# Attention's end, the MLP's first and its last period: bit steps, sums, splits and second-layer products in another order

## The chip, the core and the metric

One core of a Trainium2 chip runs the whole program in one launch. The metric is the time of one execution in microseconds of device time, the median of several runs. The engines have queues of their own and run in the order in which their instructions were written down: TensorE (PE in the profile) multiplies matrices, VectorE (DVE) and ScalarE (ACT) read what it leaves in PSUM, GpSimd (POOL) works on SBUF alone here, and SyncE (SP) issues the transfers. They wait for each other by semaphores that are set when the program is built.

## What is computed

Clustered attention, then a gated layer (MLP), then a mixture of four experts. The part that the change touches is the border between the first two and the whole of the gated layer:

```
x    = attention output, 1536 tokens x 512
gate = 1 / (1 + exp(-(x @ w_gate)))          w_gate, w_val: 512 x 1536, given in float64
val  = x @ w_val
y    = (gate * val) @ w_out                  w_out: 1536 x 512, float64
then   out = sum over 4 experts of p_e * (relu(y @ w1[e]) @ w2[e])
```

## The kernel before, in words

Every number that TensorE multiplies is split into a high part (rounded to fp32r) and a low part, the rest; a product is high x high + high x low + low x high. ACT mostly makes the high part by a copy and POOL or DVE the low part by a subtraction (`split`). The float64 weights come as pairs of 32-bit words. ACT takes a scaled magnitude of the upper word and converts the lower one (`mag`, L687 and L689), DVE does three bit steps (`bits`: clamp L694, shift L695, merge of the sign L696), and POOL adds the rounding (`round`, L701).

The gated layer runs in six periods p (NP = 6) of 256 hidden columns, for the batches b = 0 and 1. One gate or one value product of a 512 x 256 weight block with a batch's 512 x 768 operand is done by seven products of half-size blocks in place of eight (`seven`, L810 to 868), which need four sums of weight blocks (`sums`, L736) and four sums of operand blocks (t1 to t4). They are issued in the order 1, 6, 7, 5, 2, 4, 3, six matmuls of 384 columns each. There are four PSUM banks for them: product 1 and later 2 lie in the first, 6 and later 4 in the second, 7 in the third, 5 and later 3 in the fourth. L843 (u2) reads the second bank and sets it free for product 4; L851 reads the fourth and lets product 3 add to it; L860 and L865 finish products 4 and 3. The results leave in `evict`: for the gate a sigmoid on ACT (L902), for the value a multiplication by the gate on DVE (L914), then the high part G on ACT (L915) and its low part on POOL (L916). The second layer, `outp` (L920 to 962), multiplies G with two outer blocks of w_out (`part`, L925 to 929), f = 0 and 1, into four banks per half n of a batch, and adds each to acc (L937 to 941). With `soon` its first half interleaves the four banks.

Between two steps of a `seven`, and behind every evict of an `outp`, stands a place for other work: the lists given to `gate`, `value` and `outp` in `moe1` (L966 to 1046) are taken one entry per place, and so set by hand the order on ACT, DVE and POOL. In attention the same is done by tables, of which TAIL (L73) holds the steps behind the last of the 96 score blocks' places: the number is the place, counted back from the end. In it `t1` is the first operand sum of batch 1 (POOL, L554, tile tB), `bits10` and `bits11` are the bit steps of the two halves of the first value weights (tile cv), `round10` and `round11` their roundings, `xadd6` and `xscale6` add and scale the last but one pair's output (POOL, L534 and L538, tile R), and `sums1` and `t2` follow. In the last period `ys` and `ysplit` (`operands`, L1053 to 1068) make the four sums and the seven splits of the mixture's first operand, out of acc: sums on DVE (L1066), high parts on ACT (L1063), low parts on DVE (L1064).

Of the kernel before, what the change touches and what calls it, by code (L numbers as in the profile page):

```python
# [28 lines left out]
def r2(ap):  # L29
# [48 lines left out]
    "table": (-3, 2),  # L78
# [3 lines left out]
class Net:  # L82
# [801 lines left out]
    def moe1(self, xadd, xscale):  # L884
        nc = self.nc
        NP = F1 // 256
# [33 lines left out]
        def outp(p, b, work=(), soon=False):  # L920
# [3 lines left out]
            def part(ps, d, c, f, some=range(3)):  # L924
                dc = slice(d * 128, d * 128 + 128)  # L925
                t = self.outers[2 * p + f]
                for k in some:
                    x, y = (("hi", Gh), ("lo", Gh), ("hi", Gl))[k]
                    nc.tensor.matmul(ps, t[x][:, dc], y[:, f, c], start=f == 0 and k == 0, stop=f == 1 and k == 2)  # L929
# [16 lines left out]
            for n in range(2):  # L946
                c = slice(n * HB, n * HB + HB)
                if soon and n == 0:
                    banks = [bank() for _ in range(4)]
                    for some in ((0, 1), (2,)) if p in (0, NP - 1) else (range(3),):  # L950
                        for d in range(4):
                            part(banks[d], d, c, 0, some)
                    for d in range(4):
                        part(banks[d], d, c, 1)
                        evict(banks[d], d, n)
                else:
                    for d in range(4):
                        ps = bank()
                        part(ps, d, c, 0)
                        part(ps, d, c, 1)  # L960
                        evict(ps, d, n)
# [14 lines left out]
        def total(u):  # L976
            return [lambda: u["sums"](Q)]
# [8 lines left out]
        split0(2, V)  # L986
        gate(0, 0, [[vs[0], o0["split"]], [vs[1]] + d[0], [vs[2]] + d[1], [vs[3]] + d[2], d[3] + d[4], [], [xadd, xscale]])
        go = load(U[1][0])
# [5 lines left out]
        c, d = conv(U[1][0], 0), conv(U[1][0], 1)  # L994
        gate(0, 1, [c[0], c[1], c[2], c[3] + c[4] + d[0], d[1] + d[2], d[3] + d[4], total(U[1][0])])
        outers[2]["load"]()
        value(0, 1, [load(U[1][1])] + [[go] for go in U[1][0]["split"]])
        for p in range(1, NP):
# [18 lines left out]
            outp(p, 0, [d[0], d[1], d[2], d[3] + d[4], total(g), [split[0]], [], [split[1]]], soon=True)  # L1017
            value(p, 1, [load(U[p + 1][1]), [split[2]], [split[3]]])
        f = 2 * NP - 1
# [3 lines left out]
        self.load_in2(0)  # L1023
        c, e = conv(o0), conv(o1)
        outp(NP - 2, 1, [[vs[1], vs[0]], [vs[2]] + c[0], c[1], c[2], c[3] + c[4], [vs[3]] + e[0], e[1] + e[2], e[3] + e[4]])
        self.load_out2(0)
        self.load_in2(1)
        value(NP - 1, 0, [[o0["split"]], [o1["split"]]])
        out, cin = self.conv_out2(0), self.conv_in2(0)
# [7 lines left out]
        ys, ysplit = self.operands(0, [room(self.opx, t, F32) for t in ("h1", "l1", "h2", "l2")])  # L1037
        gate(NP - 1, 1, [[ys[0]], [ys[1]], [ys[2]], [lambda: ysplit(0)], [], [], [lambda: ysplit(4)]])
        Y[6] = room(self.xp, "tA"), room(self.xp, "tB")
        value(NP - 1, 1, [[cin[1]], [cin[2], lambda: ysplit(5)], [], [], [], [], [ys[3], lambda: ysplit(3)]])  # L1040
        self.late2 = late = self.conv_in2(1)
# [234 lines left out]
```

## Time and profile before

| what | value |
|---|---|
| median of 3 runs | 1051.17 us (1050.76 to 1051.79) |
| the profiled execution | 1050.76 us, its span 1048.8 us |
| TensorE | 1030.3 us busy, 98% |
| VectorE | 815.6 us, 78% |
| GpSimd | 626.0 us, 60% |
| ScalarE | 542.7 us, 52% |
| granted TensorE clock, mean | 0.996 of full speed |

The span runs from the first to the last instruction; the execution's time holds some 2 us more around it. Busy shares are means over stages of different kinds: attention ends at about 258 us, the gated layer lies between there and 545 us, and the mixture behind it. Where TensorE is busy nearly all the time, another engine's work matters where TensorE waits for it.

### The profile page before, as it was taken

How to read it: one execution, taken by the hardware profiler on the slowest of the kernel's cores; microseconds unless marked ns; L12 is line 12 of the kernel's file. 1: busy time of each engine (PE TensorE's matmuls, PEld its weight loads, DVE VectorE, ACT ScalarE, POOL GpSimd, SP SyncE). 2: the span in 40 equal slices, each digit the busy share in tenths (PEclk: the TensorE clock that was granted, in tenths of full speed). 3: DMA queues.
4: the chain of work that ended last, by engine and by line, in shares of the span. 5: the costliest groups of instructions: out<-in, count | busy, mean ns of one | idle time of the engine just before them, and what ended most of it. 6: DMA issues, size and time to landing. Idle time of an engine off the chain costs nothing.

```text
span 1048.8 us, 16255 instructions
## 1 busy us (share of the span) xinstructions
PE 1030.3 (98%) x5817; PEld 963.0 (92%) x5817; DVE 815.6 (78%) x1418; ACT 542.7 (52%) x1147; POOL 626.0 (60%) x577
## 2 busy tenths in 40 slices
PE   7999999998999999999999999999999999999998
PEld 7899999998999999999999899899899889989987
DVE  7899999899887777787787776776777876676675
ACT  5889989889654444444344333333343433333320
POOL 6676777988576868676758444444444644444430
PEclk8999999999999999999999999999999999999999
DMA  9668978563122222222212221221213221221201
GB/s 197 148 157 190 209 163 180 140 166 94 51 62 66 74 82 60 62 61 65 77 41 81 81 68 55 81 81 41 81 61 122 81 81 44 77 81 61 61 21 61
DMA packets 86544, 95.96 MB, mean 91 GB/s; under 512 B 42752, under 2 KB 59488, under 8 KB 86464
## 3 DMA queue, kind: packets, MB, share of 16 engines
q1 hardware_dynamic: 86320, 94.89, 34.0%
q8 instruction: 46, 0.75, 0.3%
q14 instruction: 34, 0.28, 0.1%
q10 hardware_dynamic: 144, 0.03, 0.0%
HBM read 65.07 MB, written 3.19 MB: 65 GB/s over the span
## 4 chain that ended last, share of the span: by engine, by line
PE 84%; DVE 6%; POOL 4%; issue 2%; ACT 2%; SPq 1%; DMA 0%; DVEq 0%; POOLq 0%; ACTq 0%
PE ph L830 34%; PE po L1143 8%; PE po L1144 8%; PE po L1142 8%; PE po L929 7%; PE S L456 5%; PE T L476 5%; PE PV L489 3%; PE PV L490 3%; PE sn L311 1%; PE sT L293 1%; PE T L269 1%; POOL G L916 1%; DVE ph L865 1%; DVE sg L914 1%
## 5 line engine op out<-in xcount | busy, mean ns | idle before, releaser
L1098 POOL TENSOR_TENSOR wol<-r,woh 128x512 fp32r<-128x512 f32 x62 | 80.1, 1294 | 151.9 <-ACT woh L1097 151.7
L1149 DVE SCALAR_TENSOR_TENSOR acc<-po,pn,acc 128x512 f32<-128x512 f32 (+1 forms) x181 | 129.8, 742 | 36.2 <-PE po L1144 36.2
L1144 PE MATMUL po<-woh,h2l 128*128 128x512 f32 (+1 forms) x374 | 145.6, 389 | 0.0
L1143 PE MATMUL po<-wol,h2h 128*128 128x512 f32 (+1 forms) x374 | 145.6, 389 | 0.0
L1142 PE MATMUL po<-woh,h2h 128*128 128x512 f32 (+1 forms) x374 | 145.0, 388 | 0.0
L748 POOL TENSOR_TENSOR w1l<-sf,w1h 128x512 fp32r<-128x512 f32 x88 | 114.9, 1326 | 43.5 <-ACT w1h L745 43.3
L1117 ACT ACTIVATE h2h<-ph 128x384 fp32r<-128x384 f32 x128 | 62.5, 490 | 119.5 <-PE ph L830 93.4
L830 PE MATMUL ph<-h,w1h 128*128 128x384 f32 x336 | 113.8, 339 | 1.2 <-ACT sg L902 0.6
L830 PE MATMUL ph<-h,w1l 128*128 128x384 f32 x336 | 112.7, 336 | 0.0
L830 PE MATMUL ph<-l,w1h 128*128 128x384 f32 x336 | 112.6, 335 | 0.0
L480 DVE TENSOR_TENSOR pl<-T,ph 128x384 fp32r<-128x384 f32 x192 | 97.6, 549 | 16.7 <-ACT ph L479 15.8
L929 PE MATMUL po<-G,woh 128*128 128x384 f32 x384 | 101.5, 337 | 2.3 <-POOL G L916 1.6
L1118 DVE SCALAR_TENSOR_TENSOR h2l<-ph,h2h 128x384 fp32r<-128x384 f32 x128 | 71.0, 554 | 34.4 <-ACT h2h L1117 31.2
L745 ACT ACTIVATE w1h<-sf 128x512 fp32r<-128x512 f32 x86 | 54.3, 632 | 83.5 <-DVE sf L736 68.8
L748 POOL TENSOR_TENSOR w1l<-r,w1h 128x512 fp32r<-128x512 f32 x64 | 67.8, 1060 | 46.8 <-ACT w1h L745 46.8
L456 PE MATMUL S<-R,L 80*128 80x384 f32 (+1 forms) x384 | 92.7, 363 | 0.9 <-ACT P L467 0.9
L459 DVE TENSOR_REDUCE nm<-S 128x1 f32<-128x768 f32 x96 | 91.1, 949 | 2.1 <-PE S L456 1.2
L479 ACT ACTIVATE ph<-T 128x384 fp32r<-128x384 f32 x192 | 84.1, 493 | 15.6 <-PE T L476 15.5
L467 ACT ACTIVATE P<-S,nm 128x768 f32<-128x768 f32 x96 | 87.7, 914 | 2.5 <-DVE nm L459 2.5
L476 PE MATMUL T<-ident,P 128*128 128x128 f32 x576 | 81.3, 276 | 3.8 <-DVE pl L480 3.0
L1144 PEld LDWEIGHTS po<-woh,h2l 128*128 128x128 f32 x374 | 70.2, 188 | 14.5
L1142 PEld LDWEIGHTS po<-woh,h2h 128*128 128x128 f32 x374 | 70.2, 188 | 13.9
(296 smaller groups left out, 2754.9 us busy)
## 6 DMA issues: line engine op xcount, KB each, us to landing
r<-in_moe_w_dram SPq DMA_DIRECT2D x64, 512.0 KB, 4.0
L<-hiq SPq DMA_DIRECT2D x32, 192.0 KB, 4.7
R<-hik SPq DMA_DIRECT2D x32, 192.0 KB, 4.7
raw<-in_moe_w_val_dram SPq DMA_DIRECT2D x12, 512.0 KB, 3.7
rwo<-in_moe_w_out_dram SPq DMA_DIRECT2D x10, 512.0 KB, 3.4
raw<-in_moe_w_gate_dram SPq DMA_DIRECT2D x10, 512.0 KB, 3.6
L<-loq SPq DMA_DIRECT2D x16, 192.0 KB, 3.6
R<-lok SPq DMA_DIRECT2D x16, 192.0 KB, 5.3
```

What stands on the lines that cost most here:

```text
L456: nc.tensor.matmul(ps[:, a, 0:384], l[0:k, c], r[0:k, a * 384:a * 384 + 384], start=l is L1, stop=l is L2)
L459: nc.vector.tensor_reduce(nm, ps[:, :, 0:384], axis=AX.XY, op=ALU.max, negate=True)
L467: nc.scalar.activation(r2(pt), ps[:, :, 0:384], AF.Exp, bias=nm, scale=1.0, accum_out=P["sums"][:, i, 0:1])
L476: nc.tensor.transpose(ps[:, j, :], pt[:, c:c + 128], self.ident)
L480: nc.vector.tensor_tensor(lo, ps, hi.bitcast(F32), op=ALU.subtract)
L748: nc.gpsimd.tensor_tensor(lo[:, sl], x, hi[:, sl].bitcast(F32), op=ALU.subtract)
L830: nc.tensor.matmul(ps, x[:, a, j], y[:, j], start=first and j == 0 and k == 0, stop=j == 1 and k == 2, skip_group_check=not first)
L929: nc.tensor.matmul(ps, t[x][:, dc], y[:, f, c], start=f == 0 and k == 0, stop=f == 1 and k == 2)
L1142: nc.tensor.matmul(ps, Hh[:, f, c], wh[:, dc], start=f == 0, stop=False)
L1143: nc.tensor.matmul(ps, Hh[:, f, c], wl[:, dc], start=False, stop=False)
L1144: nc.tensor.matmul(ps, Hl[:, f, c], wh[:, dc], start=False, stop=f == 1)
L1149: nc.vector.scalar_tensor_tensor(a, ps, pe, a, op0=ALU.mult, op1=ALU.add)
```

## The change

No work is added or taken away; instructions change their places, and two low parts change their engine.

- TAIL: `t1` moves from place -8, ahead of `bits10`, to -5, behind `round11`.
- First gate seven: magnitude and all three bit steps of the second outer block o1 stand at the first place, with the split of the value weights' first part; the split of o0 moves to the fifth.
- `outp` with `soon` in the first and last period: the f = 1 products with the high part of G for two banks go ahead of the first one with its low part.
- Second gate seven: the second half's shift step moves one place back.
- `value` of the last but one period, batch 1: it takes the conversion of the last period's first outer block; the `outp` behind it has the other block's alone, and o0's split at its end.
- Last gate seven: all four sums stand at its first place (three of them were spread), and the splits 0 and 3 at the second, their low parts on POOL in place of DVE.

```diff
--- before.py
+++ after.py
@@ -73,8 +73,8 @@
 TAIL = {
     "open": (-12, 0), "load10": (-12, 0), "load11": (-12, 0), "sums0": (-12, 2), "outer1": (-11, 2),
     "split00": (-11, 2), "split01": (-11, 2), "split02": (-10, 2), "split03": (-10, 2),
-    "mag10": (-8, 2), "t1": (-8, 2), "bits10": (-7, -7, -7), "round10": (-7, 1), "xadd6": (-6, 0), "mag11": (-6, 2),
-    "bits11": (-5, -5, -5), "round11": (-5, 1), "xscale6": (-5, 2), "sums1": (-4, 2), "t2": (-3, 2),
+    "mag10": (-8, 2), "bits10": (-7, -7, -7), "round10": (-7, 1), "xadd6": (-6, 0), "mag11": (-6, 2),
+    "bits11": (-5, -5, -5), "round11": (-5, 1), "t1": (-5, 2), "xscale6": (-5, 2), "sums1": (-4, 2), "t2": (-3, 2),
     "table": (-3, 2),
 }
 
@@ -947,12 +947,19 @@
                 c = slice(n * HB, n * HB + HB)
                 if soon and n == 0:
                     banks = [bank() for _ in range(4)]
-                    for some in ((0, 1), (2,)) if p in (0, NP - 1) else (range(3),):
+                    if p in (0, NP - 1):
+                        for f, some, d in [(0, (0, 1), d) for d in range(4)] + [(0, (2,), d) for d in range(4)] + \
+                                [(1, (0, 1), 0), (1, (0, 1), 1)] + \
+                                [x for d in range(4) for x in [(1, (2,), d)] + [(1, (0, 1), d + 2)] * (d < 2)]:
+                            part(banks[d], d, c, f, some)
+                            if f == 1 and some == (2,):
+                                evict(banks[d], d, n)
+                    else:
                         for d in range(4):
-                            part(banks[d], d, c, 0, some)
-                    for d in range(4):
-                        part(banks[d], d, c, 1)
-                        evict(banks[d], d, n)
+                            part(banks[d], d, c, 0)
+                        for d in range(4):
+                            part(banks[d], d, c, 1)
+                            evict(banks[d], d, n)
                 else:
                     for d in range(4):
                         ps = bank()
@@ -984,7 +991,8 @@
         split0(1, V)
         split0(6, Q)
         split0(2, V)
-        gate(0, 0, [[vs[0], o0["split"]], [vs[1]] + d[0], [vs[2]] + d[1], [vs[3]] + d[2], d[3] + d[4], [], [xadd, xscale]])
+        gate(0, 0, [d[0] + d[1] + d[2] + d[3] + [vs[0]], [vs[1]], [vs[2]], [vs[3]] + d[4], [o0["split"]], [],
+                    [xadd, xscale]])
         go = load(U[1][0])
         value(0, 0, [[go[0]], [o1["split"]], [go[1]], [], [], [],
                      [lambda: sums["t2"](slice(1, 2), V), lambda: sums["t3"](eng=V), lambda: split(0, V)]])
@@ -992,7 +1000,8 @@
                     [lambda: sums["t4"](eng=V), lambda: split(1, V)], [lambda: split(6, V)], [lambda: split(2, V)]],
              soon=True)
         c, d = conv(U[1][0], 0), conv(U[1][0], 1)
-        gate(0, 1, [c[0], c[1], c[2], c[3] + c[4] + d[0], d[1] + d[2], d[3] + d[4], total(U[1][0])])
+        gate(0, 1, [c[0], c[1], c[2], c[3] + c[4] + d[0], d[1], d[2] + d[3] + d[4],
+                    total(U[1][0])])
         outers[2]["load"]()
         value(0, 1, [load(U[1][1])] + [[go] for go in U[1][0]["split"]])
         for p in range(1, NP):
@@ -1015,17 +1024,18 @@
             gate(p, 1, [e[0], e[1], e[2], e[3] + e[4], [o1["split"]] + c[0], c[1] + c[2], c[3] + c[4]])
             outers[2 * p + 2]["load"]()
             outp(p, 0, [d[0], d[1], d[2], d[3] + d[4], total(g), [split[0]], [], [split[1]]], soon=True)
-            value(p, 1, [load(U[p + 1][1]), [split[2]], [split[3]]])
+            c = conv(outers[2 * p + 2]) if p + 2 == NP else [[]] * 5
+            value(p, 1, [load(U[p + 1][1]), [split[2]] + c[0], [split[3]], c[1], c[2], c[3] + c[4]])
         f = 2 * NP - 1
         o1 = outers[f] = self.outer(f, self.raw.tile([128, 2, 256], I64, name="raw", tag="raw"),
                                     self.cv.tile([128, 2, 512], F32, name="of", tag="cv")[:, 0])
         o1["load"]()
         self.load_in2(0)
-        c, e = conv(o0), conv(o1)
-        outp(NP - 2, 1, [[vs[1], vs[0]], [vs[2]] + c[0], c[1], c[2], c[3] + c[4], [vs[3]] + e[0], e[1] + e[2], e[3] + e[4]])
+        e = conv(o1)
+        outp(NP - 2, 1, [[vs[1], vs[0]], [vs[2]], [vs[3]] + e[0], e[1], e[2], e[3], e[4], [o0["split"]]])
         self.load_out2(0)
         self.load_in2(1)
-        value(NP - 1, 0, [[o0["split"]], [o1["split"]]])
+        value(NP - 1, 0, [[o1["split"]]])
         out, cin = self.conv_out2(0), self.conv_in2(0)
         outp(NP - 1, 0, [[lambda: cin[0](Q)], [], [out[0]], [], [out[1]]], soon=True)
         self.load_out2(1)
@@ -1035,9 +1045,9 @@
         Y[1], Y[2] = (t[:, 0], t[:, 1]), (t[:, 2], t[:, 3])
         self.Y = Y
         ys, ysplit = self.operands(0, [room(self.opx, t, F32) for t in ("h1", "l1", "h2", "l2")])
-        gate(NP - 1, 1, [[ys[0]], [ys[1]], [ys[2]], [lambda: ysplit(0)], [], [], [lambda: ysplit(4)]])
+        gate(NP - 1, 1, [list(ys), [lambda: ysplit(0, Q), lambda: ysplit(3, Q)], [], [], [], [], [lambda: ysplit(4)]])
         Y[6] = room(self.xp, "tA"), room(self.xp, "tB")
-        value(NP - 1, 1, [[cin[1]], [cin[2], lambda: ysplit(5)], [], [], [], [], [ys[3], lambda: ysplit(3)]])
+        value(NP - 1, 1, [[cin[1]], [cin[2], lambda: ysplit(5)]])
         self.late2 = late = self.conv_in2(1)
         outp(NP - 1, 1, [[cin[3]], [lambda: ysplit(1)], [cin[4]], [lambda: late[0](Q)], [lambda: ysplit(6)], [],
                          [late[1]]], soon=True)
```

POOL at attention's end: tB is `t1`, the two cv are the roundings, the first R is `xadd6`, the second `xscale6`. Before:

```order
L748 TENSOR_TENSOR w1l<-R_62,w1h 128x256
L554 TENSOR_TENSOR tB<-R_62 128x768
L701 TENSOR_TENSOR cv<-cv,raw 128x512
L534 TENSOR_TENSOR R_62<-A,W 128x768
L701 TENSOR_TENSOR cv<-cv,raw 128x512
L538 TENSOR_TENSOR R_62<-R_62,rb 128x768
L736 TENSOR_TENSOR sf<-cv 128x256
```

With the change:

```order
L748 TENSOR_TENSOR w1l<-R_62,w1h 128x256
L701 TENSOR_TENSOR cv<-cv,raw 128x512
L534 TENSOR_TENSOR R_62<-A,W 128x768
L701 TENSOR_TENSOR cv<-cv,raw 128x512
L554 TENSOR_TENSOR tB<-R_62 128x768
L538 TENSOR_TENSOR R_62<-R_62,rb 128x768
L736 TENSOR_TENSOR sf<-cv 128x256
```

The sum tB went from the place ahead of the first rounding to the one behind the second, ahead of the scaling.

DVE in the value seven of the last but one period's second batch (co is the outer block o0, whose steps stood in the `outp` a period half later). Before:

```order
L851 TENSOR_TENSOR ph_6437<-u_6414,ph_6447 128x384
L914 TENSOR_TENSOR sg<-sg,ph_6437 128x384
L914 TENSOR_TENSOR sg<-sg,ph_6415 128x384
L860 TENSOR_TENSOR ph_6467<-u_6414,ph_6467 128x384
L865 TENSOR_TENSOR ph_6447<-u_6413,ph_6447 128x384
L914 TENSOR_TENSOR sg<-sg,ph_6467 128x384
L914 TENSOR_TENSOR sg<-sg,ph_6447 128x384
```

With the change:

```order
L851 TENSOR_TENSOR ph_6440<-u_6414,ph_6450 128x384
L914 TENSOR_TENSOR sg<-sg,ph_6440 128x384
L694 TENSOR_SCALAR co<-co 128x512
L914 TENSOR_TENSOR sg<-sg,ph_6415 128x384
L695 TENSOR_SCALAR co<-co 128x512
L860 TENSOR_TENSOR ph_6472<-u_6414,ph_6472 128x384
L696 SCALAR_TENSOR_TENSOR co<-rwo,co 128x512
L865 TENSOR_TENSOR ph_6450<-u_6413,ph_6450 128x384
L914 TENSOR_TENSOR sg<-sg,ph_6472 128x384
L914 TENSOR_TENSOR sg<-sg,ph_6450 128x384
```

A bit step now stands behind each of the first L914, the second L914 and L860.

DVE in the last gate seven (the sums' tiles are h_6826, l_6827, h_6828 and l_6829; l_6818 is a low part). Before:

```order
L1066 TENSOR_TENSOR h_6826<-acc_4136 128x768
L843 TENSOR_TENSOR u_6832<-m_6831,ph_6843 128x384
L1066 TENSOR_TENSOR l_6827<-acc_4136,h_6826 128x768
L847 TENSOR_TENSOR u_6833<-u_6832,ph_6852 128x384
L1066 TENSOR_TENSOR h_6828<-l_6827,acc_4136 128x768
L851 TENSOR_TENSOR ph_6852<-u_6833,ph_6861 128x384
L1064 TENSOR_TENSOR l_6818<-acc_4136,h_6817 128x768
L860 TENSOR_TENSOR ph_6879<-u_6833,ph_6879 128x384
```

With the change:

```order
L1076 TENSOR_TENSOR h_6826<-acc_4136 128x768
L1076 TENSOR_TENSOR l_6827<-acc_4136,h_6826 128x768
L1076 TENSOR_TENSOR h_6828<-l_6827,acc_4136 128x768
L1076 TENSOR_TENSOR l_6829<-l_6827,acc_4136 128x768
L843 TENSOR_TENSOR u_6832<-m_6831,ph_6846 128x384
L847 TENSOR_TENSOR u_6833<-u_6832,ph_6858 128x384
L851 TENSOR_TENSOR ph_6858<-u_6833,ph_6866 128x384
L860 TENSOR_TENSOR ph_6882<-u_6833,ph_6882 128x384
```

The four sums stand together ahead of L843, and the low part l_6818 is gone from this queue. It is found on POOL, with l_6820, between the mixture's first outer and first inner weights:

```order
L1108 TENSOR_TENSOR wo_6775<-r_6663,wo_6775 128x512
L1108 TENSOR_TENSOR wo_6788<-r_6663,wo_6788 128x512
L1074 TENSOR_TENSOR l_6818<-acc_4136,h_6817 128x768
L1074 TENSOR_TENSOR l_6820<-h_6826,h_6819 128x768
L748 TENSOR_TENSOR w1l<-r_6577,w1h 128x512
L748 TENSOR_TENSOR w1l<-sf,w1h 128x512
```

Both stand where POOL went from wo to w1l directly.

## Rows read from the trace of the kernel before

**Rows 1.** Busy time by stretch, the sum over 243:258, 258:338, 487:519 and 519:545 us.

```profile
sum 153.00, PE 145.86 PEld 138.66 DVE 124.37 ACT 87.45 POOL 101.89; mean PE 36.47 PEld 34.67 DVE 31.09 ACT 21.86 POOL 25.47
```

**Rows 2.** Chain of waits: start us, us, what; one half of a second-layer block.

```profile
333.60 4.16 PE po L929 x24
```

**Rows 3.** Timeline of TensorE, early: start us, us, what [idle before <- releaser].

```profile
247.27 0.55 PE L476 MATMUL T<-ident,P 128*128 128x128 f32 x3 [1.78 <-DVE pl L480]
...
257.12 0.44 PE L476 MATMUL T<-ident,P 128*128 128x128 f32 x2 [0.24 <-DVE pl L480]
...
267.01 0.33 PE L830 MATMUL ph<-h,w1h 128*128 128x384 f32 x1
...
270.91 0.44 PE L830 MATMUL ph<-h,w1h 128*128 128x384 f32 x1 [0.59 <-ACT sg L902]
...
280.36 0.61 PE L929 MATMUL po<-G,woh 128*128 128x384 f32 x2 [0.48 <-POOL G L916]
...
295.47 0.44 PE L830 MATMUL ph<-g,w1h 128*128 128x384 f32 x1 [0.38 <-ACT sg L902]
```

**Rows 4.** Timeline of TensorE, from the last but one period's end on.

```profile
490.70 0.44 PE L830 MATMUL ph<-h,w1h 128*128 128x384 f32 x1
...
501.70 0.44 PE L929 MATMUL po<-G,woh 128*128 128x384 f32 x1 [0.33 <-DVE acc L941]
...
516.22 0.96 PE L929 MATMUL po<-G,woh 128*128 128x384 f32 x4 [0.79 <-POOL G L916]
...
528.49 0.33 PE L830 MATMUL ph<-A,w1h 128*128 128x384 f32 x1
...
532.22 0.44 PE L830 MATMUL ph<-g,w1h 128*128 128x384 f32 x1 [0.29 <-ACT sg L902]
...
542.68 0.62 PE L929 MATMUL po<-G,woh 128*128 128x384 f32 x2 [0.35 <-POOL G L916]
```

**Rows 5.** Timeline of DVE at attention's end.

```profile
243.73 1.83 DVE L694 TENSOR_SCALAR cv<-cv 128x512 f32<-128x512 f32 x1
...
250.26 0.42 DVE L694 TENSOR_SCALAR cv<-cv 128x512 f32<-128x512 f32 x1
...
251.17 0.69 DVE L696 SCALAR_TENSOR_TENSOR cv<-raw,cv 128x512 int32<-128x512 int32 x1
...
255.37 1.22 DVE L566 TENSOR_TENSOR l<-R,h 128x768 fp32r<-128x768 f32 x1
256.52 1.01 DVE L480 TENSOR_TENSOR pl<-T,ph 128x384 fp32r<-128x384 f32 x2
```

**Rows 6.** Timeline of POOL, attention's end and the value seven at 482 us.

```profile
243.44 1.84 POOL L554 TENSOR_TENSOR tB<-R 128x768 f32<-128x768 f32 x1
...
253.25 1.84 POOL L538 TENSOR_TENSOR R<-R,rb 128x768 f32<-128x768 f32 x1
255.04 0.74 POOL L736 TENSOR_TENSOR sf<-cv 128x256 f32<-128x256 f32 x1
255.86 1.32 POOL L736 TENSOR_TENSOR sf<-sf,cv 128x256 f32<-128x256 f32 x1
...
486.64 2.53 POOL L748 TENSOR_TENSOR w1l<-sf,w1h 128x512 fp32r<-128x512 f32 x2
```

**Rows 7.** Timeline of ACT in the first gate seven.

```profile
264.61 0.49 ACT L496 ACTIVATE U<-PV 128x384 f32<-128x384 f32 x1 [0.57 <-PE PV L490]
264.99 0.67 ACT L687 ACTIVATE co<-rwo 128x512 f32<-128x512 f32 x1
```

**Rows 8.** Timeline of DVE: second gate seven, the value seven at 482 us, last gate seven.

```profile
294.00 0.43 DVE L695 TENSOR_SCALAR cv<-cv 128x512 int32<-128x512 int32 x1
...
487.18 1.02 DVE L914 TENSOR_TENSOR sg<-sg,ph 128x384 f32<-128x384 f32 x2
...
523.96 0.95 DVE L1066 TENSOR_TENSOR h<-acc 128x768 f32<-128x768 f32 x1
```

**Rows 9.** Timeline of ACT in the last gate seven.

```profile
524.53 0.49 ACT L839 ACTIVATE m<-ph 128x384 f32<-128x384 f32 x1 [7.94 <-PE ph L830]
...
529.35 0.84 ACT L1063 ACTIVATE h<-acc 128x768 fp32r<-128x768 f32 x1
```

## The prediction

> **What bounds the kernel now.** The first view is the page's busy shares: TensorE is busy in 98% of the span, so the change can win only pauses of TensorE. The second, busy time by stretch, shows how much there is in the four stretches that the change touches: 153.00 us with 145.86 us of TensorE work [rows 1], so 7.1 us at the very most, of which an edit can add more as well as take some. The chain of waits gives the unit: a run of 24 products takes 4.16 us [rows 2], 0.173 us each, and each term below is how far TensorE's row of products is moved. The third view is TensorE's timeline, where a bracket shows each pause and what ended it [rows 3, 4]. The last are the timelines of VectorE (DVE) and GpSimd (POOL) side by side, and they show what the pauses come from. The clamp L694 of one weight half takes 1.83 us at 243.73 and 0.42 us at 250.26 [rows 5]. In the first case POOL's sum tB ran from 243.44 to 245.28 [rows 6] and the clamp ended 0.28 us after it. The low part L566, which reads two SBUF tensors, was issued at 255.37 and ended at 256.59 [rows 5], 0.81 us after the sum sf that POOL had begun at 255.04; the next sf was issued at 255.86, took 1.32 us in place of 0.74, and ended 0.59 us after DVE [rows 6]. So these two engines take turns on such instructions. Whoever waits already is served at the end of the other's instruction, also where both have more queued. PSUM readers such as pl (1.01 us for two) keep their time beside POOL [rows 5].
>
> **Attention's end.** The sum t1 (tB) leaves the place in front of the clamp. The clamp then takes 0.42 us and DVE, which has no idle time from 243 to 257, is 1.41 us earlier; the pause of 1.78 us at 247.27 [rows 3] shrinks by that. But t1 now stands behind the second rounding, and the scaling R behind t1. R now starts right behind that rounding, at 253.25 for 1.84 us [rows 6]. Shifted by 1.41, t1 takes this place, 251.84 to 253.68, and R comes after it, to 255.48. DVE issues L566 at 253.96 and must wait for R: it ends at 255.48 + 0.81 = 256.29, only 0.31 before its old end. The pair pl behind it frees the bank for the transpose at 257.12 [rows 3], and behind that the next pause stands only at 270.91. Term: -0.3; bounds -1.4 (no wait) and 0.
>
> **First gate seven.** A seven issues seven products of six matmuls; the sixth needs the bank that the second filled, freed by L843. All three bit steps now stand in front of L843. They need the magnitude co, which ACT starts at 264.99 and ends at 265.66, right behind the attention's last copy U [rows 7]; with the shift of 0.3 that is 265.35. POOL's low parts wait for ACT behind it, so the steps run free: 0.42 + 0.43 + 0.69 us and three gaps [rows 5], to 267.0, and L843 ends near 267.5. The sixth product stood at 267.01 [rows 3], with the shift at 266.7: a new pause of 0.8 us. In return L860 no longer stands behind the bits, and the pause at 270.91 (0.59 us idle, 0.76 beyond the cadence) goes: the second product of the value seven starts at 270.74. Term: +0.1; bounds -0.7 and +0.9. The moved split of o0 costs nothing: its low part is wanted only at 277, and POOL has it by 275.3.
>
> **Second-layer products and the second gate seven.** The pause at 280.36 [rows 3] waits for the third low part of G. Four products now go in front of it, 0.35 us of its 0.48. But DVE and ACT set when the next gate seven hands over its banks, and those stay, so I count none of it. There, the second bit step (0.43 us, 294.00 [rows 8]) moves behind L860; the sigmoid behind L860 frees the bank for the product at 295.47, so its pause of 0.38 us goes, with restart 0.45. Term: -0.45; bounds -0.8 and -0.1. The first half of the change is then -0.3 + 0.1 - 0.45 = -0.6 (rounded).
>
> **The last period's outer weights.** Magnitude, bits and rounding of o0 move into the value seven at 482 to 490. There POOL works through four low parts of weights without a break (486.64, 2.53 us for two [rows 6]). The clamp comes at 487.65, behind the first of L914's two [rows 8], and ends at the boundary 487.92 + 0.28 = 488.2; the shift step waits for the next low part, 489.35 + 0.28 = 489.63, and the merge step for one more. L860 slips from 488.6 to 489.55, L914 behind it from 490.1 to 491.16, and TensorE's product at 490.70 [rows 4] moves to 491.76: +1.06. The same turns delay the bits of the weights in the next gate seven, so that the bank at 501.70 [rows 4] comes 1.43 us late. What is gained: DVE has only one set of bits left in the layer after it, POOL reaches G earlier, and the pause of 0.79 us at 516.22 [rows 4], waiting for G, goes, with 0.46 just ahead of it. The ninth second-layer product then starts at 516.07, where it stood at 516.22, and 0.2 us is lost at the next G. Term: +0.1; bounds -1.2 (the three steps meet no low part) and +1.4 (nothing is given back).
>
> **The last gate seven.** Four sums of 0.95 us now stand in front of L843, from 523.96 [rows 8] to 527.8 if nothing disturbs them; L843 would end at 528.3, in time for the sixth product at 528.49 [rows 4]. But ACT's high part of acc is moved forward too, right behind m (524.53, 0.49 us); at 0.84 us [rows 9] it ends at 525.76, and POOL, which was idle here, issues the low part at 525.83, while DVE's second sum still runs (to 525.90). So POOL goes next. A POOL instruction of this size takes 1.84 us [rows 6], and after a wait about 1.68 (1.84 less the 0.15 that the sf row lost): to 527.58. The third sum ends at 528.39, POOL's second low part at 530.07, the fourth sum at 530.88, L843 at 531.35, and the sixth product starts at 531.40: a pause of 2.9 us. What goes: 0.29 idle (0.57 with restart) at 532.22, some 0.15 before it, and the 0.35 idle (0.62 with restart) at 542.68 [rows 4], where DVE's fourth sum and low part had slowed POOL's G. Term: 2.9 + 0.1 - 1.4 = +1.6; bounds -1.4 (no pause) and +2.4 (nothing won later).
> The Trainium skill, Perfetto Trace Analysis, "Optimizing Scalar/DVE Operations", says that GpSimd's port is VectorE's second pair and that offloading between these two might not help. By it the low parts put on POOL would win nothing, which is what the sum has.
>
> **Sum.** -0.6 + 0.1 + 1.6 = +1.1 us. The profiled execution took 1050.76 us (span 1048.8), the fastest of three; their median lies 0.41 above it. I add the sum to the median 1051.17: **1052.3 us**, no change that a measurement can tell (0.2% is 2.1 us).
>
> **Rivals.** *POOL comes too late for its turn.* The margin is 525.83 against the third sum's issue at 525.93. If DVE takes the third sum first, only the fourth waits, L843 ends at 529.83 and the pause is 1.4: the last term is 0.1, the sum -0.4, 1050.8 us. For it speaks the small margin; against it, that both times hang on the same run of products.
> *The moved steps fall beside POOL's instructions.* If R is done before L566 (-1.4 in place of -0.3), the outer weights' steps meet no low part (-1.2 in place of +0.1) and POOL is late as above, the sum is -0.4 - 1.1 - 1.3 = -2.8: 1048.4 us. For it: a shift of 0.5 us in POOL's queue changes each turn. Against it: POOL has no gap at 254 and 488 [rows 6].
> *Sums with two SBUF inputs do not wait.* Then R holds nothing up, -1.4, and the last gate seven only wins, -1.4: the sum is 1.1 - 1.1 - 3.0 = -3.0, 1048.2 us. Against it stands L566 at 255.37 [rows 5]. The skill's page named above speaks of a 2-port operation alone as what holds the port, which would be this case; its page SBUF — State Buffer, "Who interferes with whom", adds a VectorE instruction with two SBUF inputs, and the trace agrees with that (0.81 us behind POOL).
> *The loss at 490 to 502 is not given back* (the slower side). Its place is the ninth product of the last period's first second-layer block. If POOL ends its second G later than 516.07, as it does now (516.2), TensorE keeps the late bank's 1.4 us: -0.6 + 1.4 + 1.6 = +2.4, 1053.6 us. For it: the pause of 0.79 us shows how late POOL is there now [rows 4]. Against it: one rounding leaves that queue.
>
> **How the numbers follow.** Forecast 0.50, POOL too late 0.12, steps beside POOL 0.17, no waits for two inputs 0.07, loss not given back 0.14. The first two are no change, 0.62; faster 0.24; slower 0.14. The range runs from 1048.0, just below the two faster cases, to 1053.8, just above the slower one; the forecast's own, with POOL too late, from 1050.8 to 1053.2.
>
> **What would show it.** In the new profile the clamp at 242 to 244 takes 0.42 us and L566 behind it ends 0.81 us after R; TensorE pauses 0.8 us before the first gate seven's sixth product, about 1.3 us ahead of the last period's first gate seven's second product, and 2.9 us before the last gate seven's sixth, released by L843, with the third and fourth sum at 2.4 us each. If those two sums take 0.95, the largest term is wrong; if L860 near 488.6 is on time, the outer weights' term is.

## The result and the profile after

The changed kernel took 1057.2 us, the median of six executions (1055.69 to 1059.53); the kernel before had 1050.97 beside it. The ratio is 1.0059 (95% interval 1.0046 to 1.0072): **slower by 6.2 us** (4.8 to 7.6), where 1052.3 was forecast, in a range that ended at 1053.8. The profiled execution took 1058.71 us, its span 1056.8; that is 8.0 more than before. Experiments were compared with the kernel before in the same sitting, whose median was 1052.2 there, so their ratios count, not their medians; 0.1% is 1.05 us.

TensorE does the same 5817 matmuls. What is 8.0 us longer is seen in its timeline, which answers to [rows 3, 4]:

```profile
241.09 0.34 PE L489 MATMUL PV<-ph,vv 128*128 128x384 f32 x1
...
246.83 0.55 PE L476 MATMUL T<-ident,P 128*128 128x128 f32 x3 [0.37 <-DVE pl L480]
...
257.77 0.55 PE L476 MATMUL T<-ident,P 128*128 128x128 f32 x3 [1.34 <-DVE pl L480]
...
268.54 0.41 PE L830 MATMUL ph<-h,w1h 128*128 128x384 f32 x1 [0.74 <-DVE u L843]
...
272.14 0.33 PE L830 MATMUL ph<-h,w1h 128*128 128x384 f32 x1
...
278.34 0.44 PE L830 MATMUL ph<-h,w1h 128*128 128x384 f32 x1 [1.88 <-DVE u L843]
...
284.81 0.33 PE L929 MATMUL po<-G,woh 128*128 128x384 f32 x1
...
309.43 0.44 PE L830 MATMUL ph<-nk,w1l 128*128 128x384 f32 x1 [0.34 <-POOL w1l L748]
...
496.54 0.44 PE L830 MATMUL ph<-h,w1h 128*128 128x384 f32 x1 [1.15 <-DVE sg L914]
...
507.94 0.44 PE L929 MATMUL po<-G,woh 128*128 128x384 f32 x1 [0.71 <-DVE acc L941]
...
520.89 1.03 PE L929 MATMUL po<-G,woh 128*128 128x384 f32 x5
...
536.31 0.69 PE L830 MATMUL ph<-A,w1h 128*128 128x384 f32 x1 [2.83 <-DVE u L843]
...
550.71 0.33 PE L929 MATMUL po<-G,woh 128*128 128x384 f32 x1
```

The same matmul is looked up in both traces, and the difference of its starts is how late TensorE is there: 246.83 against 247.27 is -0.44, 257.77 against 257.12 is +0.65, 272.14 against 270.91 +1.23, 284.81 against 280.36 +4.45, 520.89 against 516.22 +4.67, 550.71 against 542.68 +8.03. At 241.09, ahead of the first changed instruction, it is already +0.97. Two of these rows before:

```profile
240.12 0.34 PE L489 MATMUL PV<-ph,vv 128*128 128x384 f32 x1
...
304.75 0.45 PE L830 MATMUL ph<-nk,w1l 128*128 128x384 f32 x1
```

The profiles of the experiments show between +0.06 and +1.74 at this matmul, with or without each part of the change; this first 1.0 us is left out below.

| step | forecast | profile |
|---|---|---|
| attention's end | -0.3 | 0.97 to 0.65: -0.3 |
| first gate seven | +0.1 | 0.65 to 1.23: +0.6 |
| value seven, second-layer products, second gate seven | -0.45 | 1.23 to 4.68 (at 309.43): +3.45 |
| the last period's outer weights | +0.1 | 4.68 to 4.67: 0.0 |
| last gate seven | +1.6 | 4.67 to 8.03: +3.4 |

Two pauses carry it: 1.88 us before the first value seven's sixth product, which nothing in the forecast had, and 2.83 us before the last gate seven's sixth, which it had. Busy time by stretch shows what stands behind each (the column after POOL is the granted clock):

```profile
276.00:280.00 4.00, 2.11 (x11) 1.47 (x10) 3.72 (x6) 0.00 (x0) 0.02 (x1) 1.00 0.10 42
280.00:283.40 3.40, 3.40 (x12) 3.33 (x11) 2.78 (x7) 1.58 (x4) 1.98 (x2) 0.50 0.00 0
...
532.00:536.00 4.00, 1.48 (x9) 1.16 (x7) 4.00 (x3) 0.00 (x0) 2.98 (x2) 1.00 0.00 0
536.00:539.40 3.40, 3.09 (x10) 3.09 (x11) 1.94 (x4) 1.04 (x3) 0.00 (x0) 0.50 0.00 0
```

For 3.4 us behind each pause TensorE runs at half clock, 1.2 GHz. At 280 it starts 12 products where it would have started some 20 (3.4 / 0.173), at 536 it starts 10 in the 3.09 us that are busy, where there would have been 18: about 1.4 us, for each pause. Its busy time does not show this loss: in the first of the two stretches TensorE counts as busy throughout.

What made the pauses is on DVE and POOL. DVE:

```profile
254.92 2.32 DVE L566 TENSOR_TENSOR l<-R,h 128x768 fp32r<-128x768 f32 x1
...
274.81 2.02 DVE L534 TENSOR_TENSOR R<-A,W 128x768 f32<-128x768 f32 x1 [3.10 <-POOL wol L806]
...
277.74 0.55 DVE L843 TENSOR_TENSOR u<-m,ph 128x384 f32<-128x384 f32 x1
...
530.76 2.55 DVE L1076 TENSOR_TENSOR h<-l,acc 128x768 f32<-128x768 f32 x1
533.24 2.55 DVE L1076 TENSOR_TENSOR l<-l,acc 128x768 f32<-128x768 f32 x1
535.71 0.54 DVE L843 TENSOR_TENSOR u<-m,ph 128x384 f32<-128x384 f32 x1
```

and POOL:

```profile
254.60 1.83 POOL L538 TENSOR_TENSOR R<-R,rb 128x768 f32<-128x768 f32 x1
...
273.48 1.29 POOL L806 TENSOR_TENSOR wol<-R,woh 128x512 fp32r<-128x512 f32 x1
274.73 1.29 POOL L806 TENSOR_TENSOR wol<-co,woh 128x512 fp32r<-128x512 f32 x1
...
530.66 1.84 POOL L1074 TENSOR_TENSOR l<-acc,h 128x768 fp32r<-128x768 f32 x1 [1.91 <-ACT h L1073]
532.46 2.52 POOL L1074 TENSOR_TENSOR l<-h,h 128x768 fp32r<-128x768 f32 x1
```

The sum L534 of attention's last pair stood idle for 3.10 us until POOL's low part of o0, `wol<-R`, ended at 274.77. The name of that operand tells why: o0's converted block lies in R1[:,2560:3072], and the last pair's output, which L534 writes, takes R1[:,2304:3072]. The sum may not write before the low part has read. When DVE was let go, POOL had already begun the next one, so L534 took its turn behind it as well (2.02 us, 0.81 behind 276.02). Before, o0's low part was done at 265.65 and L534 began at 270.71, right behind L865:

```profile
264.35 1.30 POOL L806 TENSOR_TENSOR wol<-R,woh 128x512 fp32r<-128x512 f32 x1
```

```profile
270.71 1.38 DVE L534 TENSOR_TENSOR R<-A,W 128x768 f32<-128x768 f32 x1
```

### The profile page after: what moved, and what is told of

The parts are those of the page before. It is cut to its first block, busy times and chain, and to the rows that moved or that the text cites. A ratio compares the mean times of both kernels' runs of the same rounds, so it can differ in the third digit from the quotient of the medians.

```text
span 1056.8 us, 16256 instructions
## 1 busy us (share of the span) xinstructions
PE 1033.5 (98%) x5817; PEld 965.9 (91%) x5817; DVE 815.1 (77%) x1416; ACT 543.2 (51%) x1147; POOL 629.0 (60%) x579
## 4 chain that ended last, share of the span: by engine, by line
PE 85%; DVE 6%; POOL 4%; issue 3%; ACT 1%; DMA 0%; SPq 0%; POOLq 0%; DVEq 0%; ACTq 0%
PE ph L830 34%; PE po L929 9%; PE po L1154 8%; PE po L1153 8%; PE po L1152 8%; PE S L456 5%; PE T L476 5%; PE PV L489 3%; PE PV L490 3%; PE sn L311 1%; PE sT L293 1%; POOL w1l L748 1%; PE T L269 1%; DVE sg L914 1%; DVE ph L865 1%
## 5 line engine op out<-in xcount | busy, mean ns | idle before, releaser
L1153 PEld LDWEIGHTS po<-wol,h2h 128*128 128x128 f32 x374 | 70.2, 188 | 13.9
```

What stands on the lines that cost most here:

```text
L1153: nc.tensor.matmul(ps, Hh[:, f, c], wl[:, dc], start=False, stop=False)
```

## The experiments

The expectations count a pause from start to start, less the usual step: they have 2.04, 3.0 and 1.53 us where the brackets of the rows have 1.88, 2.83 and 1.34.

**Each half put back.** First o0's split alone:

```diff
-gate(0, 0, [d[0] + d[1] + d[2] + d[3] + [vs[0]], [vs[1]], [vs[2]], [vs[3]] + d[4], [o0["split"]], [],
+gate(0, 0, [d[0] + d[1] + d[2] + d[3] + [vs[0], o0["split"]], [vs[1]], [vs[2]], [vs[3]] + d[4], [], [],
```

> The changed kernel with one step put back: o0's split at the first place of the first gate seven. Theory (the last pair's sum L534 overwrites the place in tile R where o0's converted block lies, so it waits for o0's low part wol<-R, which the change put last in POOL's queue; TensorE's clock falls behind the long pause that follows): L534 starts within 1.5 us of L865's end, the pause of 2.04 us before the first value seven's sixth product at 278.3 goes to under 0.3 us, no granted clock of 0.5 at 280 to 283.4; in all 3.3 to 3.8 us less than the changed kernel, about 1053.6 us. Rival A (POOL's queue as such is too full there, whichever order): the pause stays between 1.5 and 2.5 us and the time at 1057. Rival B (the slow clock comes at its hour and not behind a pause): pause gone, but 3.4 us at half clock still at about 280; 2 us less, 1055.2 us.

Measured 1.0029 (1.0019 to 1.0039), 3.2 us less than the changed kernel; the theory's 3.3 to 3.8 lies within the intervals. DVE and, below it, two stretches:

```profile
270.69 2.05 DVE L534 TENSOR_TENSOR R<-A,W 128x768 f32<-128x768 f32 x1
...
274.08 0.54 DVE L843 TENSOR_TENSOR u<-m,ph 128x384 f32<-128x384 f32 x1
```

```profile
280.00:283.40 3.40, 3.40 (x21) 3.40 (x21) 3.40 (x3) 2.58 (x6) 2.30 (x2) 1.00 0.02 5
531.40:534.80 3.40, 2.86 (x9) 2.86 (x10) 2.14 (x5) 0.87 (x2) 0.00 (x0) 0.50 0.00 0
```

L534 starts without idle time, the pause is gone, and so is the half clock at 280: 21 products in the 3.4 us that held 12. Nine products are 1.6 us. The half clock behind the other pause is still there. Rivals A and B fall.

Then the last gate seven alone:

```diff
-gate(NP - 1, 1, [list(ys), [lambda: ysplit(0, Q), lambda: ysplit(3, Q)], [], [], [], [], [lambda: ysplit(4)]])
+gate(NP - 1, 1, [[ys[0]], [ys[1]], [ys[2]], [lambda: ysplit(0)], [], [], [lambda: ysplit(4)]])
-value(NP - 1, 1, [[cin[1]], [cin[2], lambda: ysplit(5)]])
+value(NP - 1, 1, [[cin[1]], [cin[2], lambda: ysplit(5)], [], [], [], [], [ys[3], lambda: ysplit(3)]])
```

> The changed kernel with the last gate seven put back as before (sums spread over its places, low parts 0 and 3 on DVE). Theory (turns of DVE and POOL make the pause of 3.0 us before the sixth product, and the clock falls behind it): pause gone, no half clock at 536, 3.0 to 3.6 us less than the changed kernel, about 1053.8 us; everything before 520 us as in the changed kernel, the half clock at 280 too. Rival A (the gain behind the pause is larger than booked): under 2 us less, above 1055.2. Rival B (half clock at its hour): a stretch at half clock still near 536, about 1.5 us less, 1055.7.

Measured 1.0034 (1.0022 to 1.0046), 2.6 us less. The late pause is gone and TensorE runs at full clock from 535 to 540, which rules rival B out; the early pause (1.89) and its half clock are as in the changed kernel. The size lies under the 3.0 that the theory wanted, inside the two intervals, and the medians alone do not rule out rival A (under 2 us). The profile speaks against it: from the last period's second-layer products to the next ones TensorE's row goes from +4.52 to +4.14, 3.7 us less than the changed kernel's +3.4.

Both together:

> Both put back: o0's split early and the last gate seven as before; what is left of the change is t1's place, the bit steps of o1 together, the second-layer order, the second gate seven's shift step and the last period's outer weights. Theory (the two effects add): 6.5 to 7.2 us less than the changed kernel, 1050.0 to 1050.7 us, no change against the kernel before that can be measured, no half clock after the start. Rival (the rest of the change costs too, for example its first 250 us, where the profiled run stood 1.0 us late): 1052 us or above.

Measured 0.9994 (0.9983 to 1.0005): no difference. These are the edits of the two diffs above. The two halves account for the loss: 0.30% and 0.25% singly, 0.65% together, the sum of the two within the intervals. TensorE's row stands at -0.03 at the products that had +8.03. What is left of the change wins or loses nothing that shows; the rival, that its first 250 us cost something, falls.

**The last gate seven: the sums, or the turns?** All four sums stay in front, and the two splits come three places later:

```diff
-[list(ys), [lambda: ysplit(0, Q), lambda: ysplit(3, Q)], [], [], [], [], [lambda: ysplit(4)]]
+[list(ys), [], [], [lambda: ysplit(0, Q), lambda: ysplit(3, Q)], [], [], [lambda: ysplit(4)]]
```

> The changed kernel, in whose last gate seven all four sums stay at the first place, while the splits 0 and 3 (low parts still on POOL) come three places later, behind L851. Theory (POOL's two low parts, which come between the sums, hold them up): the third and fourth sum take 0.95 us each in place of 2.55, L843 is done some 3.2 us earlier, the pause of 3.0 us is at most 0.3 us and no half clock follows; what POOL does later costs up to 1 us at G; 2.5 to 4.5 us less than the changed kernel, 1052.7 to 1054.7. Rival (the four sums themselves, 3.8 us ahead of L843, are what is too much): the pause stays above 2 us, and the time within 1 us of 1057.2.

Measured 1.0035 (1.0022 to 1.0048), 2.5 us less. DVE:

```profile
530.76 0.96 DVE L1076 TENSOR_TENSOR h<-l,acc 128x768 f32<-128x768 f32 x1
531.63 0.95 DVE L1076 TENSOR_TENSOR l<-l,acc 128x768 f32<-128x768 f32 x1
532.50 0.55 DVE L843 TENSOR_TENSOR u<-m,ph 128x384 f32<-128x384 f32 x1
```

The third sum starts at the same 530.76, takes 0.96 in place of 2.55, and the pause before the sixth product is gone. So the four sums by themselves fit; POOL's two low parts between them do not. The Trainium skill, SBUF — State Buffer, "Who interferes with whom", says that GpSimd and VectorE share one port pair that one of them holds at a time, and these two runs agree with it (2.55 against 0.96 us for the same sum). The edit gained 2.5 us of the 4.2 that the pause and the clock had cost, because a new wait took their place, on ACT and then TensorE:

```profile
534.86 0.83 ACT L1073 ACTIVATE h<-acc 128x768 fp32r<-128x768 f32 x1
535.59 0.83 ACT L1073 ACTIVATE h<-h 128x768 fp32r<-128x768 f32 x1
536.32 1.24 ACT L902 ACTIVATE sg<-ph 128x384 f32<-128x384 f32 x3
```

```profile
536.85 0.45 PE L830 MATMUL ph<-g,w1h 128*128 128x384 f32 x1 [1.11 <-ACT sg L902]
```

The splits' two high parts now stand ahead of the sigmoid that frees a bank, at 0.83 us each. The rival falls.

**The pause and the clock, apart.** On top of o0's early split, only one low part stands behind the sums:

```diff
-[list(ys), [lambda: ysplit(0, Q), lambda: ysplit(3, Q)], [], [], [], [], [lambda: ysplit(4)]]
+[list(ys), [lambda: ysplit(0, Q)], [], [], [], [lambda: ysplit(3, Q)], [lambda: ysplit(4)]]
```

> To part the pause from the slow clock behind it: as the run with o0's split early (ratio to the kernel before 1.0029), but in the last gate seven only the low part 0 stands behind the sums, the low part 3 five places behind them. Theory (each POOL low part that comes between the sums costs one turn of 1.6 us, and the clock falls behind the long pause alone): the third sum takes 2.55 us, the fourth 0.95, the pause before the sixth product is 1.3 to 1.5 us in place of 3.0 and no half clock follows, since none followed the pauses of 0.9 to 1.5 us seen so far; 2.9 to 3.3 us less than with o0's split early alone, so 0.0 to 0.4 us slower than the kernel before. Rival A (half clock follows this pause too): pause 1.4 with 3.4 us of half clock behind it, only 1.6 us less, 1.5 us slower than before. Rival B (both sums wait for the same low part, or the fourth waits for another instruction): pause above 2.

Measured 0.9999 (0.9991 to 1.0008), 3.2 us less than with both low parts there. DVE, TensorE and the stretch behind the pause:

```profile
527.35 2.55 DVE L1076 TENSOR_TENSOR h<-l,acc 128x768 f32<-128x768 f32 x1
529.82 0.95 DVE L1076 TENSOR_TENSOR l<-l,acc 128x768 f32<-128x768 f32 x1
```

```profile
531.28 0.44 PE L830 MATMUL ph<-A,w1h 128*128 128x384 f32 x1 [1.22 <-DVE u L843]
```

```profile
531.00:535.00 4.00, 3.71 (x20) 3.38 (x20) 2.47 (x5) 2.35 (x6) 0.67 (x1) 1.00 0.00 0
```

One turn costs 1.6 us, and taking one away shortens the pause from 2.83 to 1.22. That is 1.6 us. The rest is put down to the clock, which stays at full speed behind the shorter pause: 1.6 us by the ratios, whose intervals are nearly as wide, and 1.0 by the profiles, where TensorE's row moves by +3.25 across the last gate and value sevens with both low parts there and by +0.65 with one. Rival A (1.0014) lies outside the interval, rival B's pause above 2 did not come.

**Each half alone in the kernel before.**

```diff
-gate(0, 0, [[vs[0], o0["split"]], [vs[1]] + d[0], [vs[2]] + d[1], [vs[3]] + d[2], d[3] + d[4], [], [xadd, xscale]])
+gate(0, 0, [[vs[0]], [vs[1]] + d[0], [vs[2]] + d[1], [vs[3]] + d[2], d[3] + d[4] + [o0["split"]], [], [xadd, xscale]])
```

> The kernel before with one step of the change alone: o0's split at the fifth place of the first gate seven in place of the first. Theory (this move alone is enough): L534 waits 2 to 3.5 us for o0's low part wol<-R, a pause of 1.5 to 2.5 us before the first value seven's sixth product, 3.4 us of half clock behind it; 2.5 to 3.6 us slower than the kernel before. Rival (it needs the bit steps of o1 at the first place too, which load POOL's and DVE's queues in another order): pause under 0.8 us, no half clock, under 1 us slower.

Measured 1.0008 (0.9999 to 1.0017): **a miss**. DVE and TensorE:

```profile
273.67 2.04 DVE L534 TENSOR_TENSOR R<-A,W 128x768 f32<-128x768 f32 x1 [2.05 <-POOL wol L806]
```

```profile
277.22 0.45 PE L830 MATMUL ph<-h,w1h 128*128 128x384 f32 x1 [1.00 <-DVE u L843]
```

The wait for `wol<-R` is there, 2.05 us, but the pause is 1.00 and the clock does not fall. The moved split alone is not the whole cause; by itself it costs 0.8 us (-0.1 to 1.8). In the changed kernel o1's magnitude and bits stand ahead of the value weights' first split, too; POOL's four low parts of these weights began at 267.44 there and at 264.83 here, though TensorE's row was later here (+1.74 against +0.97 at 240 us). By these rows it is o1's magnitude and bits in front that make 1.00 a pause of 1.88, while with o0's split early they make none there. This is argued and not shown: the changed kernel also has t1 in another place, and no run has the moved split and the bits alone.

The last gate seven's change in the kernel before, with the lines of the second diff above the other way round:

> The kernel before with the last gate seven's change alone (all four sums at its first place, low parts 0 and 3 on POOL at the second). Theory (this alone is enough, and nothing earlier matters to it): third and fourth sum 2.4 to 2.6 us each, pause 2.9 to 3.1 us before the sixth product, half clock for 3.4 us behind it; 3.0 to 3.5 us slower than the kernel before. Rival (the turn of POOL hangs on the earlier shift of 4.7 us, as a small margin of 0.1 us let fear): only the fourth sum waits, pause 1.4, no half clock, within 0.5 us of before.

Measured 1.0023 (1.0014 to 1.0031), 2.4 us (1.5 to 3.3), most of it below the theory's 3.0 to 3.5. In its profile the sums take 2.55 us each, the pause is there with half clock behind it (0.54 from 533.0 to 536.7), and TensorE's row goes from +1.88 at 518.10 to +5.20 at 547.88, by 3.3, as in the changed kernel. So the mechanism doesn't hang on what comes earlier. The executions' median is lower than this one profile tells, as it was with the last gate seven put back; a possible reason stands in the last section.

**Can the first part be kept and bettered?** The sum t1 goes behind the scaling and the sums sf, on top of both halves put back:

```diff
-... "round11": (-5, 1), "t1": (-5, 2), "xscale6": (-5, 2), "sums1": (-4, 2), ...
+... "round11": (-5, 1), "xscale6": (-5, 2), "sums1": (-4, 2), "t1": (-4, 2), ...
```

> As the run with both put back (ratio 0.9994), with the sum t1 behind the scaling and the four sums sf of the weights in POOL's queue, ahead of t2. Theory (L566 lost to R what the clamp won, as DVE's instructions with two SBUF inputs wait for POOL's running instruction, and sf of 0.74 us costs a smaller turn than R's or t1's 1.84): L566 ends near 255.3 in place of 256.3, TensorE's pause of 1.53 us there goes to 0.4 to 0.7, 0.8 to 1.2 us less than with both put back: ratio 0.998 to 0.9985. Rival (L566 waits for whichever instruction stands in POOL's queue, or t1 now holds up the next pair's low parts by as much): no change, ratio 0.999 to 1.000.

Measured 0.9986 (0.9976 to 0.9996): faster than both kernels, by 1.5 us against the one before. Against the run with both put back (0.9994) the gain is the 0.8 us expected, but the two intervals overlap. DVE and TensorE:

```profile
255.32 1.22 DVE L566 TENSOR_TENSOR l<-R,h 128x768 fp32r<-128x768 f32 x1
```

```profile
257.06 0.55 PE L476 MATMUL T<-ident,P 128*128 128x128 f32 x3 [0.25 <-DVE pl L480]
```

L566 takes 1.22 in place of 2.32 and the pause behind it is 0.25 in place of 1.34, somewhat more than expected: what the changed kernel's clamp won, L566 lost to the scaling.

The same move alone in the kernel before:

```diff
-"mag10": (-8, 2), "t1": (-8, 2), "bits10": (-7, -7, -7), ...
+"mag10": (-8, 2), "bits10": (-7, -7, -7), ...
...
-... "xscale6": (-5, 2), "sums1": (-4, 2), "t2": (-3, 2),
+... "xscale6": (-5, 2), "sums1": (-4, 2), "t1": (-4, 2), "t2": (-3, 2),
```

> The kernel before with the sum t1 alone moved, behind the scaling and the sums sf as in the run with t1 later. Theory (the clamp no longer waits, L566 keeps its 1.22 us, and the long pause at 247.27, behind which one profiled run showed 3.41 us at half clock, is gone): TensorE's row 1.3 to 1.5 us earlier at 257, and the mean granted clock of the runs above that of before (0.9966); ratio 0.9978 to 0.9987, that is 1.4 to 2.3 us less. Rival A (the slow clock at 250 in that one run was chance): mean granted clock as before, ratio 0.9986 to 0.999. Rival B (the gain is given back at the first gate seven, where DVE waits for TensorE's fifth product in any case): ratio 0.9995 or above.

Measured 0.9986 (0.9975 to 0.9997). TensorE's row goes from +0.94 at 241 us to -0.48 at 246.80, and holds +0.10 at the second-layer products of 280.46: 1.4 won, 0.6 of it given back there. Rival B is thus half right in the profile, though its ratio of 0.9995 lies at the edge of the interval; theory and rival A meet at the ratio measured. With t1 moved alone the kernel is as fast as with the rest of the change beside it (0.9986 both), so that rest adds nothing that shows. The executions' mean granted clock was 0.9979, that of the kernel before in the same sitting 0.9971, too little to settle it.

The run with t1 later, and its first gate seven as before:

```diff
-gate(0, 0, [d[0] + d[1] + d[2] + d[3] + [vs[0], o0["split"]], [vs[1]], [vs[2]], [vs[3]] + d[4], [], [],
-            [xadd, xscale]])
+gate(0, 0, [[vs[0], o0["split"]], [vs[1]] + d[0], [vs[2]] + d[1], [vs[3]] + d[2], d[3] + d[4], [], [xadd, xscale]])
```

> Put together from what the runs showed: of the change the second-layer order, the second gate seven's step and the outer weights of the last period; t1 behind the sums sf; the first gate seven and the last one as before. Theory: -1.4 at attention's end and no pause of 0.9 us before the first gate seven's sixth product (instead 0.6 idle before the value seven's second), so 0.2 to 0.6 us less than the run with t1 later (0.9986): ratio 0.998 to 0.9985. Rival (the bits in that place cost the G behind the value seven as much): 0.9986 to 0.999.

Measured 0.9990 (0.9979 to 1.0001): in the rival's range, though the interval holds the theory's too. The bits of o1 together or spread make no difference that shows. And this one with the sums in front in the last gate seven, and the splits behind them:

```diff
-gate(NP - 1, 1, [[ys[0]], [ys[1]], [ys[2]], [lambda: ysplit(0)], [], [], [lambda: ysplit(4)]])
+gate(NP - 1, 1, [list(ys), [], [], [], [], [lambda: ysplit(0, Q), lambda: ysplit(3, Q)], [lambda: ysplit(4)]])
-value(NP - 1, 1, [[cin[1]], [cin[2], lambda: ysplit(5)], [], [], [], [], [ys[3], lambda: ysplit(3)]])
+value(NP - 1, 1, [[cin[1]], [cin[2], lambda: ysplit(5)]])
```

> As the run put together, with the four sums in front in the last gate seven and the splits 0 and 3 five places behind them, low parts on POOL. Theory (no POOL instruction of this kind between the sums, and the sigmoids are issued ahead of the splits' high parts): sums of 0.95 us, no pause before the sixth product, none of 1.3 us before the value seven's first products either; the waits of 0.3 us each at 532 and 543 go; 0.3 to 0.9 us less than the run put together. Rival (POOL's low parts, begun at 533, hold up w1l and G): a pause of 0.5 us or more before the second-layer products at 543, 0 to 1 us more.

Measured 0.9993 (0.9983 to 1.0003): the gain that the theory wanted is not there. The sums kept their 0.95 us, but at 538.31 TensorE waited 1.02 us for DVE's L851: the low parts of the splits 4 and 5 on DVE took 2.27 and 1.58 us beside POOL's moved ones and the weights' behind them. That is the rival's kind of wait, at an earlier place. The turns were only put off, not spared.

## Why the prediction was wrong

Every sign that the prediction names came true, the pauses and sums within 0.2 us; the loss lies above all in what it put at nothing.

**Attention's end** held: the clamp took 0.43, L566 waited for the scaling and ended 0.81 us behind it (256.43 and 257.24), net -0.3. The step with t1 later shows the bound of -1.4 that was kept for it.

**First gate seven**: the pause was 0.74 (forecast 0.8). The gain at 270.91 was sized too large by 0.5: +0.6 in place of +0.1.

**"The moved split of o0 costs nothing: its low part is wanted only at 277, and POOL has it by 275.3."** This is the step that failed. POOL had it at 274.77. But it asked only who reads the result, and not who waits for the operand's place. The term put at nothing is +3.2 in TensorE's row (1.23 to 4.45), the pause of 1.88 and the half clock behind it; with the split back in its place, the time fell by 3.2 us and both were gone. Moved alone in the kernel before, it cost 0.8 us.

**Second-layer products and second gate seven**: in the changed kernel TensorE's row went from +4.45 at 284.81 to +4.23 at 299.70, half of the -0.45, and back to +4.68 at 309.43. With both halves put back, TensorE's row went from +0.30 at 271.21 to -0.08 at 295.39, the -0.4 forecast, and lost it at 305.12, where it stood at +0.37 behind a wait of 0.37 us for POOL's low part of the weights. The forecast had stopped at 295.

**Outer weights**: right in each step: from +4.68 to +5.84 at 496.54 (490.70 before) and +6.24 at 507.94 (forecast +1.06 and +1.43), all given back by 520.89.

**Last gate seven**: the turns were right, though the margin of 0.1 us was thin: sums of 2.55 us each (forecast 2.4), a pause of 2.83 (2.9). What failed is the sum 2.9 + 0.1 - 1.4: it priced a pause by its length alone and had no term for the clock behind it, 1.0 to 1.6 us by the run with one low part, 1.4 by the products counted. The opening bound has the same gap: it takes idle time for all that can be won, and a product at half clock counts as busy. The trace of the kernel before shows such a case. There TensorE waited once for longer than in any later place, and the stretches behind that wait ran at 0.72 and 0.59 of full clock:

```profile
15.63 0.84 PE L398 MATMUL oT<-identb,oh 128*16 128x128 bf16 x12 [2.13 <-DVE oh L388]
```

```profile
15.00:20.00 5.00, 3.52 (x20) 2.58 (x20) 4.38 (x9) 1.79 (x3) 2.85 (x6) 0.72 0.97 223
20.00:25.00 5.00, 4.99 (x23) 4.86 (x24) 3.37 (x9) 3.63 (x9) 1.01 (x1) 0.59 1.04 229
```

The forecast did not draw on these rows, which lie far from the change. None of the rivals had the moved split or the clock in it; the slower one, that the loss at 490 to 502 is not given back, did not happen.

## What to carry to other kernels

For an instruction that is moved later, list not only who reads its result but who overwrites its operands: here the next write to the same tile waited 3.10 us for it. Before an elementwise instruction is moved from VectorE to GpSimd, see what VectorE does with SBUF operands at that moment: each such pair in the same microseconds cost one turn of 1.6 us, and moved later it cost turns in another place. Price a long pause of TensorE (1.9 us and more here) at its length and, as a likely further cost, the slow clock behind it (about 1.4 us here); look at the longest pauses in the trace, wherever they are, and at the granted clock behind them. Busy time does not show that cost.

## What the runs showed of the hardware

The clock behind a pause is no fixed matter. Behind the pauses of 1.88 to 1.90 us near 278 and of 2.83 us in the last gate seven each profile showed 1.2 GHz, three of each; behind those from 1.00 to 1.37 us, none. In between it varied. The pause at attention's end, which the kernel before has too (1.78, [rows 3]), left the clock at full speed in its profile, as did the one of 1.82 us in the run with o0's moved split alone; the run with the last gate seven's change alone has the same instructions there and shows this, TensorE's row and then the stretches:

```profile
248.55 0.55 PE L476 MATMUL T<-ident,P 128*128 128x128 f32 x3 [1.82 <-DVE pl L480]
```

```profile
245.00:250.00 5.00, 3.18 (x20) 2.91 (x20) 4.93 (x8) 3.45 (x9) 3.30 (x3) 1.00 0.01 2
250.00:253.40 3.40, 3.40 (x14) 3.30 (x14) 3.33 (x7) 3.40 (x7) 1.48 (x2) 0.50 0.56 157
```

Nor is length alone what decides. The wait of 2.13 us near 15 us stands in every profile. In eleven of the thirteen half clock follows within 2 us, for 3.4 to 10.2 us. In the run with one low part it came only behind a further pause of 1.57 us, and in the run with the last gate seven's change alone not at all:

```profile
15.41 0.84 PE L398 MATMUL oT<-identb,oh 128*16 128x128 bf16 x12 [2.13 <-DVE oh L388]
```

```profile
15.00:20.00 5.00, 3.01 (x22) 2.26 (x23) 4.68 (x11) 2.16 (x4) 2.61 (x6) 1.00 0.91 200
20.00:25.00 5.00, 4.72 (x35) 4.03 (x34) 3.96 (x9) 4.48 (x12) 2.33 (x3) 1.00 1.08 227
```

So the kernel before may pay for the pause at attention's end in some executions and not in others, and one profile may tell more or less of the clock than the median holds. That stays open: the mean granted clock of the executions points that way (0.9983 and 0.9981 in the runs with t1 later and with one low part, 0.9966 in the kernel before, of the same sitting), but the run put together, which has no such pause either, had 0.9973 against 0.9971.
